# An empty 32 bytes in front of the late part's pool of a linear-attention and two-MLP kernel

## The chip, the core and the metric

The kernel runs on one core of one Trainium2 chip. The metric is the device time of one execution in microseconds (us); a kernel's time is the median over its runs.

## The reference

Attention with a feature map, then two MLPs (multi-layer perceptrons), all in float32. Inputs: q, k and v of 4 batches, 8 heads, 576 positions and 64 values; x below has 2,304 rows of 512.

```python
proj = x @ w_phi; proj -= max|proj|
phi = concat(exp(proj), exp(-proj))
attn = (phi(q) @ (phi(k).T @ v)) / (phi(q) @ sum(phi(k)) + 1e-6)
h = attn @ w_in;   g = where(h > 0, h, exp(min(h, 0)) - 1);   x = g @ w_out
h = x @ w_in2;     g = h * cos(h);                            out = g @ w_out2
```

Both MLPs go from 512 to 2,048 and back to 512.

## The kernel before, in words

**Work.** Attention fills `xy`, the 2,304 tokens as columns of 4 pieces of 128 partitions. The MLPs work on blocks of tokens: the first half of MLP 1 on blocks of 256 columns (the early part), its second half and all of MLP 2 on blocks of 384 (the late part). The late part is 6 blocks of 8 steps and 6 blocks of 16 steps, 144 steps in all. A step (`step`) takes 128 of the 2,048 hidden values: `g1` (L697) makes them with 12 matmuls, ACT and DVE put them through the activation, and `g2` (L705) adds them to the output banks with 12 more.

**Why 12 matmuls.** Each operand is split into a high part and a low remainder that TensorE takes in one pass each (`fp32r`); a product takes three passes (high by high, high by low, low by high) over 4 pieces. The stationary operand is a weight tile (`h` or `l`). The moving operand, the one that is streamed, is `x` in `g1` and `s` in `g2`, its high half in the first 384 columns of the tile and its low half in the next 384.

**Places in SBUF.** `unit` gives each kind of tile its places. `x` has 4 (`x0` to `x3`) and `s` three (`s0` to `s2`) in the pool `mp`. From the late part on, `s` has a fourth place, `sq0`, in the pool `mq`, and in MLP 2 from about 650 us on a fifth, `sx0`, in the pool `mx`. A step's `s` goes to whichever of them is free first by the plan. `mq` also holds three places for the activation's values (`gq`), two for what is loaded or stored at a block's end (`oq`) and two of `kq` (the whole number of turns for the cosine; a third, `kx0`, lies in `mx`). `swap("at", "wb", "mq")` releases attention's pool and opens `wb` and `mq` in its place, with `mq` behind `wb`.

In the built program, by the byte at which a tile starts in each partition: `mp` and `mx` come from the right-hand end of SBUF, and their tiles lie at 32 modulo 64 (`s0` at 216,032, `sx0` at 197,088, `x0` at 201,696, `kx0` at 200,160). `mq` begins at 174,912, and its tiles lie at 0 modulo 64 (`sq0` at 179,520). A tile of `x` or `s` takes 3,072 bytes, a half of it 1,536, so that both halves lie alike. The weight tiles and `xy` lie at 0 modulo 64.

**Order.** `plan` lists all instructions ahead of time from a table of costs and due times; each engine runs its own in that order. Addresses play no part in it.

Of the kernel before, what the change touches and what calls it, by code (L numbers as in the profile page):

```python
# [8 lines left out]
F32 = mybir.dt.float32  # L9
# [14 lines left out]
P = 128  # L24
# [46 lines left out]
NL, W1LATE, NEQ, EARLY = 4, -24.05, 4, 176.41  # L71
KLOAD, VLOAD, QSTEP = 20.0, 15.0, 4.0
NO = 2
JS, NSPLIT, WGAP = 4, 0, 20.0
ND, NKF, NVT, NQF, RAWB, NE = 5, 2, 2, 2, 4, 5

# [132 lines left out]
def bits(w):  # L209

    return w.bitcast(U32).rearrange("j p i (m t) -> j p i m t", t=2)
# [7 lines left out]
def body(tc, qt, kt, vt, wphi, w1, w2, out):  # L219
    nc = tc.nc  # L220
    pools, count = {}, itertools.count()

    def pool(name, **kw):
        pools[name] = tc.alloc_tile_pool(name=name, bufs=1, **kw)
        return pools[name]

    cst, xp, dr = pool("cst"), pool("xp"), pool("dr", space=DRAM)
    pool("wa")
    pool("wc")
# [1 line left out]
    pool("mp", side="right")  # L231
    pool("stg", side="right")
    pool("at")
    ws = {1: bits(w1), 2: bits(w2)}

    xy = xp.tile([P, NK, NT], F32, tag="xy", name="xy")
# [28 lines left out]
    def task(*args, **kw):  # L265
        t = Task(*args, **kw)
        t.ready = 0.0
        tasks.append(t)
        for b in t.bufs:
            if b.places[0][0] in hold:  # L270
                hold[b.places[0][0]].append(t)
        return t
# [4 lines left out]
    def unit(kind, late, last=False, dtype=F32):  # L277
        pool_of = {"x": {"mp": 4}, "s": {"mp": 3}, "g": {"mp": 2}, "o": {"mp": NO}, "k": {}}[kind]
        size = {"x": 2 * NB, "s": 2 * NB, "g": NA, "o": 2 * NA, "k": NB}[kind]
        places = [("mp", f"{kind}{i}") for i in range(pool_of.get("mp", 0))]  # L280
        if late and kind in "go":
            places, size = [], {"g": NB, "o": 2 * NB}[kind]
        if late:
            places += [("mq", f"{kind}q{i}") for i in range({"s": 1, "g": 3, "o": 2, "k": 2}.get(kind, 0))]
        if last:
            places += [("mx", f"{kind}x{i}") for i in range({"s": 1, "k": 1}.get(kind, 0))]
        return Buf(places, [P, size], dtype)
# [473 lines left out]
    def swap(old, *new, **kw):  # L761
        def fn():
            if old:
                pools[old].release()
            for n in new:
                pool(n, **kw)

        t = task("SP", 0.0, -1e6, fn, after=hold.get(old, hold["pools"]), latency=0.001)
        t.opens = new
        hold["pools"] = [t]  # L770
# [4 lines left out]
    for b in range(B):  # L775
        keys(b, BEGIN + PACE * (b * S / NA) - LEAD - KLEAD if b else 0.0, 4.0, reached)
        while T * P + P <= (b + 1) * S:
# [3 lines left out]
            T += 1  # L781
    end_a = BEGIN + BLOCK_A * (NT // NA)
    swap("at", "wb", "mq")
    for j in range(JA, NJ):
        convert("wb" if j > JA else "wc", 1, j, end_a + W1LATE + 4.0 * (j - JA) - (0 if j > JA else EARLY))
# [13 lines left out]
    for j in range(JA, NJ):  # L799
        convert("wb" if j > JA else "wc", 2, j, due + W2LATE + 4.2 * (j - JA))  # L800
    swap("stg", "mx", side="right")
    for c0, n in late:
        block(2, 0, c0, n, due, BLOCK_C * n / 384)
# [73 lines left out]
```

## Time and profile before

| | |
|---|---|
| median of 3 runs | 1008.83 us (1008.05 to 1008.95) |
| the profiled execution | 1008.61 us |
| its span, first to last instruction | 1006.7 us |
| granted TensorE clock | 1.000 |
| TensorE (PE) busy in the span | 994.3 us (99%) |
| VectorE (DVE), ScalarE (ACT), GpSimd (POOL) busy | 716.7, 504.4, 209.5 us |

The profile is of one execution. PE is the matmuls, PEld the loading of their stationary operand. Matmuls are pipelined: one starts before the last has ended, so that the time one takes (its duration, in ns) is longer than its distance to the next one's start.

### The profile page before, as it was taken

To read this page: it belongs to the slowest core of one execution; us is meant where nothing else is said; L and a number is where in the kernel's file an instruction comes from. 1 tells how busy PE (TensorE), PEld (TensorE's weight loads), DVE (VectorE), ACT (ScalarE), POOL (GpSimd) and SP (SyncE) were. 2 spreads that over 40 slices of the span, in tenths; PEclk is the share of its full clock that TensorE was granted. 3 is DMA by queue.
4 is the path that set the end of the run, shared out by engine and by line. 5 is a ranking of instruction groups with operands and counts; after the bars stand their busy time and mean duration, and the time that the engine had idled before them with its cause. 6 is when DMAs were issued, how large, how long until landed. Compare 5 with 4: busy or idle time off the path is not lost.

```text
span 1006.7 us, 21101 instructions
## 1 busy us (share of the span) xinstructions
PE 994.3 (99%) x8422; PEld 956.3 (95%) x8422; DVE 716.7 (71%) x1424; ACT 504.4 (50%) x1196; POOL 209.5 (21%) x262
## 2 busy tenths in 40 slices
PE   9999999999999999999999999999999999999998
PEld 6787988988999999999999999999999999999998
DVE  6999977778666678996444679975666666756564
ACT  6886753555456778875232576632232332422322
POOL 3556300000003447763000255500000000000000
PEclk9999999999999999999999999999999999999999
DMA  7544212120102345341002232100000000000000
GB/s 232 176 125 134 86 49 80 33 69 17 45 13 95 105 142 169 127 141 53 2 31 74 75 104 95 43 32 1 1 33 1 1 32 1 32 1 1 32 1 32
DMA packets 45889, 63.28 MB, mean 63 GB/s; under 512 B 5728, under 2 KB 24800, under 8 KB 45792
## 3 DMA queue, kind: packets, MB, share of 16 engines
q1 hardware_dynamic: 45632, 61.88, 19.5%
q8 instruction: 66, 1.08, 0.5%
q14 instruction: 31, 0.25, 0.1%
q10 hardware_dynamic: 160, 0.07, 0.0%
HBM read 52.49 MB, written 9.44 MB: 62 GB/s over the span
## 4 chain that ended last, share of the span: by engine, by line
PE 91%; DVE 5%; issue 1%; ACT 1%; POOL 1%; DMA 0%; DVEq 0%; ACTq 0%
PE h L697 24%; PE y L705 24%; PE a L697 15%; PE a L705 15%; PE a L561 4%; PE a L389 3%; PE a L441 3%; PE a L538 1%; DVE l L354 1%; DVE m L402 1%; DVE l L350 1%; DVE ek L470 1%; DVE d L405 1%; POOL l L358 1%; PE y L448 0%
## 5 line engine op out<-in xcount | busy, mean ns | idle before, releaser
L697 PE MATMUL h<-x,h 128*128 128x256 f32 (+1 forms) x1152 | 256.3, 313 | 0.1
L705 PE MATMUL y<-s,h 128*128 128x256 f32 (+1 forms) x956 | 205.0, 306 | 0.0
L697 PEld LDWEIGHTS h<-x,h 128*128 128x128 f32 x1152 | 192.8, 188 | 5.1 <-issue 3.3
L697 PE MATMUL h<-x,l 128*128 128x256 f32 (+1 forms) x576 | 178.6, 310 | 1.4 <-POOL l L372 1.4
L358 POOL TENSOR_TENSOR l<-l,h 128x256 int32<-128x256 int32 x128 | 105.1, 828 | 304.0 <-DMA raw<-w 190.6
L705 PEld LDWEIGHTS y<-s,h 128*128 128x128 f32 x956 | 157.2, 188 | 3.5 <-issue 1.9
L697 PE MATMUL a<-x,h 128*128 128x384 f32 x576 | 148.7, 340 | 0.0
L705 PE MATMUL y<-s,l 128*128 128x256 f32 (+1 forms) x478 | 145.2, 304 | 0.0
L372 POOL TENSOR_TENSOR l<-l,h 128x256 fp32r<-128x256 f32 x128 | 106.1, 838 | 134.3 <-ACT h L369 133.5
L697 PEld LDWEIGHTS h<-x,l 128*128 128x128 f32 x576 | 108.3, 188 | 1.6 <-POOL l L372 1.6
L739 ACT ACTIVATE gq<-gq,pihalf 128x384 f32<-128x384 f32 x96 | 59.2, 617 | 95.7 <-DVE gq L736 95.7
L697 PEld LDWEIGHTS a<-x,h 128*128 128x128 f32 x576 | 104.9, 188 | 0.0
L705 PE MATMUL a<-s,h 128*128 128x384 f32 x380 | 98.1, 340 | 0.0
L697 PE MATMUL a<-x,l 128*128 128x384 f32 x288 | 97.8, 340 | 0.0
L705 PEld LDWEIGHTS y<-s,l 128*128 128x128 f32 x478 | 89.9, 188 | 0.0
L369 ACT CAST h<-l 128x256 fp32r<-128x256 f32 x128 | 51.7, 406 | 37.6 <-POOL l L358 36.9
L354 DVE SCALAR_TENSOR_TENSOR l<-raw,l 128x256 uint32<-128x256 uint32 x128 | 69.1, 553 | 1.1
L705 PEld LDWEIGHTS a<-s,h 128*128 128x128 f32 x380 | 69.2, 188 | 0.0
L705 PE MATMUL a<-s,l 128*128 128x384 f32 x190 | 64.6, 340 | 0.0
L754 DVE TENSOR_TENSOR s<-gq,s 128x384 fp32r<-128x384 f32 x95 | 58.3, 613 | 3.5 <-ACT s L253 1.1
L343 ACT ACTIVATE l<-raw 128x256 f32<-128x256 f32 x128 | 56.0, 438 | 8.7 <-DMA raw<-w 8.5
L350 DVE TENSOR_SCALAR l<-l 128x256 uint32<-128x256 uint32 x128 | 51.2, 416 | 9.4 <-ACT l L343 8.2
(112 smaller groups left out, 1670.1 us busy)
## 6 DMA issues: line engine op xcount, KB each, us to landing
raw<-w SPq DMA_DIRECT2D x128, 256.0 KB, 3.0
qf<-qt SPq DMA_DIRECT2D x18, 256.0 KB, 2.7
part<-o SPq DMA_DIRECT2D x18, 256.0 KB, 2.4
oq<-part SPq DMA_DIRECT2D x12, 384.0 KB, 3.4
out<-oq SPq DMA_DIRECT2D x12, 384.0 KB, 2.5
kf<-kt SPq DMA_DIRECT2D x16, 256.0 KB, 3.6
vt<-vt SPq DMA_DIRECT2D x16, 256.0 KB, 2.8
kf<-kt SPq DMA_DIRECT2D x4, 128.0 KB, 3.3
```

The source lines that it names most:

```text
L343: nc.scalar.activation(f.tile, raw.tile[:, :, 1].bitcast(F32), AF.Copy, scale=2.0 ** -112)
L350: nc.vector.tensor_scalar(e, e, 3, None, ALU.logical_shift_left)
L354: nc.vector.scalar_tensor_tensor(e, raw.tile[:, :, 1], 0x80000000, e, ALU.bitwise_and, ALU.bitwise_or)
L358: nc.gpsimd.tensor_tensor(e, e, r.tile, ALU.add)
L369: task("ACT", cost(ACT_, CH), due, lambda: nc.scalar.copy(h.tile, f.tile), [h], [f])
L372: nc.gpsimd.tensor_sub(l.tile, f.tile, h.tile.bitcast(F32))
L389: nc.tensor.matmul(pp[odd].tile[0:r, i * NF:(i + 1) * NF], x.tile[rows, i, 0:r], ww[rows], start=(i == 0), stop=True, skip_group_check=True,)
L561: nc.tensor.matmul(ns[odd].tile[32 * h:32 * h + 32, g * P + lo:g * P + hi], k[:, half, h // 2, at:at + 32] if g < 2 else k[:, half, 2, 32 ...
L697: nc.tensor.matmul(hp.tile[:, 0:N], columns(W[m, j, 0, kk * P // CH][a], kk), xs[kk][c](), start=(kk == 0 and n == 0), stop=(kk == NK - 1 ...
L705: nc.tensor.matmul(yp(dt), columns(W[m, j, 1, dt * P // CH][a], dt), (hi, lo)[c](), start=(i == 0 and n == 0 and (late or dt % 2 == 0)), s ...
L739: nc.scalar.activation(g.tile[:, 0:N], g.tile[:, 0:N], AF.Sin, bias=pihalf)
L754: nc.vector.tensor_sub(lo(), g.tile[:, 0:N], hi().bitcast(F32))
```

## The change

A tile of 8 float32 values (32 bytes in each partition) that nothing writes or reads is allocated in `mq` when the pool is opened.

```diff
+SHIFTED = ("mq",)
...
+    def shift(name):
+
+        pools[name].tile([P, 8], F32, tag="pad", name=f"pad_{name}")
+
...
+    if "at" in SHIFTED:
+        shift("at")
...
             for n in new:
                 pool(n, **kw)
+                if n in SHIFTED:
+                    shift(n)
```

Since `SHIFTED` has `mq` alone, attention's pool gets no pad. In the built program all tiles of `mq` start 32 bytes later (`gq0` at 174,944, `sq0` at 179,552), and so at 32 modulo 64; every other tile is where it was. The instructions of each engine stand in the same order as before, row for row.

## Rows read from the trace of the kernel before

**Rows 1.** The page: head, busy time and share of the span, instructions.
```profile
span 1006.7 us, 21101 instructions
PE 994.3 (99%) x8422; PEld 956.3 (95%) x8422; DVE 716.7 (71%) x1424; ACT 504.4 (50%) x1196; POOL 209.5 (21%) x262
```
**Rows 2.** Busy time of each engine by stretch (us from the span's start).
```profile
core 0: us, PE busy (x) PEld busy (x) DVE busy (x) ACT busy (x) POOL busy (x), PEclk, DMA share, GB/s
...
401.00:650.00 249.00, 249.00 (x1414) 249.00 (x1413) 178.52 (x344) 141.19 (x350) 97.20 (x121) 1.00 0.24 78
650.00:990.00 340.00, 340.00 (x1929) 340.00 (x1929) 215.82 (x424) 105.72 (x201) 0.00 (x0) 1.00 0.04 12
990.00:1003.00 13.00, 12.76 (x73) 12.44 (x71) 5.73 (x11) 3.38 (x7) 0.00 (x0) 1.00 0.00 0
1003.00:1006.70 3.70, 0.00 (x0) 0.00 (x0) 0.00 (x0) 0.27 (x1) 0.00 (x0) 1.00 0.57 213
```
**Rows 3.** The chain that ended last, from 395 us on, shares by line.
```profile
by line: PE h L697 24.9%; PE a L705 24.9%; PE y L705 24.9%; PE a L697 24.7%; ACT oq L253 0.1%; issue 0.0%
```
**Rows 4.** Groups by form: busy us, mean ns of one; idle before them.
```profile
L697 PE MATMUL a<-x,h 128*128 128x384 f32 x576 | 148.7, 340 | 0.0
...
L705 PE MATMUL a<-s,h 128*128 128x384 f32 x380 | 98.1, 340 | 0.0
```
**Rows 5.** Tile `sq`: durations ns min/median/max, first and last start us.
```profile
L705 PE MATMUL a<-sq,h x128: 334/334/338, 401.6 to 994.9; 128*128 128x384 f32 x128
L705 PEld LDWEIGHTS y<-sq,h x128: 187/188/188, 402.5 to 995.7; 128*128 128x128 f32 x128
L705 PE MATMUL y<-sq,h x128: 334/334/334, 402.6 to 995.9; 128*128 128x384 f32 x128
...
L754 DVE TENSOR_TENSOR sq<-gq,sq x32: 546/559/1105, 398.2 to 985.1; 128x384 fp32r<-128x384 f32 x32
L255 DVE CAST sq<-gq x20: 359/360/361, 473.7 to 984.7; 128x384 fp32r<-128x384 f32 x20
```
**Rows 6.** Tile `sx`, the same view.
```profile
L705 PEld LDWEIGHTS y<-sx,h x68: 187/188/188, 658.5 to 997.8; 128*128 128x128 f32 x68
L705 PE MATMUL y<-sx,h x68: 337/340/342, 658.6 to 998.0; 128*128 128x384 f32 x68
...
L754 DVE TENSOR_TENSOR sx<-gq,sx x17: 551/557/559, 651.8 to 989.3; 128x384 fp32r<-128x384 f32 x17
L255 DVE CAST sx<-gq x14: 359/360/361, 651.4 to 988.9; 128x384 fp32r<-128x384 f32 x14
```
**Rows 7.** PE busy with matmuls of tile `sq` alone, two stretches, their sum.
```profile
395.00:600.00 205.00, 26.95 (x144) 1.00 0.26 84
600.00:1003.00 403.00, 44.93 (x240) 1.00 0.06 20
sum 608.00, PE 71.89; mean PE 35.94
```
**Rows 8.** The same for tile `sx`.
```profile
600.00:1003.00 403.00, 38.81 (x204) 1.00 0.06 20
```
**Rows 9.** Timeline of PE: start us, us, what; first of each `g2`.
```profile
994.15 0.51 PE L705 MATMUL a<-sq,h 128*128 128x384 f32 x2
...
996.24 0.52 PE L705 MATMUL a<-sx,h 128*128 128x384 f32 x2
...
998.36 0.52 PE L705 MATMUL a<-s,h 128*128 128x384 f32 x2
...
1000.48 0.52 PE L705 MATMUL a<-s,h 128*128 128x384 f32 x2
```
**Rows 10.** Tile `gq`: durations ns min/median/max, first and last start us.
```profile
L736 DVE SCALAR_TENSOR_TENSOR gq<-kq,gq x68: 544/559/1092, 597.5 to 991.3; 128x384 f32<-128x384 int32 x68
...
L736 DVE SCALAR_TENSOR_TENSOR gq<-kx,gq x28: 551/558/559, 652.9 to 995.5; 128x384 f32<-128x384 int32 x28
```
**Rows 11.** DMA issues: xcount, KB each, median us from issue to landing.
```profile
part<-o SPq DMA_DIRECT2D x18, 256.0 KB, 2.4
...
out<-oq SPq DMA_DIRECT2D x12, 384.0 KB, 2.5
```

## The prediction

> **What bounds the kernel now.** I read the busy times first. PE works for 994.3 of 1006.7 us [rows 1]; a busy PE alone says little, so the stretches come next. The change can act only once `mq` is in use, from about 395 us on. [...] So in the late part the end moves by what the distance from one matmul to the next changes, and by nothing else, save for the last 3.7 us, in which PE does nothing and the last store goes out [rows 2].
>
> **What the change does.** It adds and removes no instruction, wait or transfer, and moves none in its queue. It moves tiles by 32 bytes: `gq`, `oq`, `kq`, and the one place of `mq` that PE streams, `sq0`. So I go by kinds of access.
>
> *PE reads of `sq`.* The trace holds the comparison already, since the same code at the same line streams from `sq` (at 0 modulo 64) and from `s`, `sx` and `x` (at 32). From `x` and `s` one matmul of 384 columns takes 340 ns [rows 4], from `sx` 340 by the median, from `sq` 334 [rows 5, 6]. The weight loads take 188 ns in both [rows 5, 6], so the 6 ns are not theirs. Duration is not pace, though, because matmuls overlap; the pace is in the stretches. The matmuls of `sq` are 384 (32 groups `g2` of 12), and PE is busy with them for 71.89 us [rows 7]: 71.89 / 32 = 2.247 us a group. Those of `sx` are 204, 17 groups, in 38.81 us [rows 8]: 2.283 us a group. The difference is 0.036 us. Each stretch ends with the tail of its last matmul, which the next group overlaps, so I check it by starts: the `sq` group begins at 994.15 and the next at 996.24, 2.09 us; the `sx` group takes from there to 998.36, 2.12 us, and the `s` group behind it again 2.12 [rows 9]. That is 0.03 us, read to 0.01. The 32 groups then cost 32 x 0.030 = 1.0 us by the starts and 32 x 0.036 = 1.2 us by the stretches. I take **1.1 us, slower**. Ends for the range: 0 if the address is not what makes `sq` quick, and 384 x 6 ns = 2.3 us if all of the longer duration showed in the pace. I choose near the middle because the pace is measured directly and the duration is not a pace.
>
> All of it lies on the path, since PE has no idle time there to take it up [rows 2]. Nor does the mixture of both kinds of place cost anything that going uniform would give back: the `sx` group just behind the `sq` group takes the same 2.12 us as the `s` group behind another place at 32 [rows 9].
>
> [...]
>
> *DVE and ACT on `sq`, `gq`, `kq`.* Writing to a place at 0 or at 32 shows no difference: L754 takes 559 ns into `sq` and 557 into `sx`, L255 360 into both [rows 5, 6]. Nor do reads, as far as rows go: L736 takes 559 ns when it reads `kq`, at 0, and 558 when it reads `kx`, at 32 [rows 10]. ACT's reads of `gq` at 32 the trace does not show. Bounds: a saving of 6 ns an instruction to a loss of the same, as PE has it. I take 0, which DVE's rows are nearest to. What covers it is the lead of these engines over PE: DVE's last instruction for `sq` starts at 398.2 us at the first use and at 985.1 at the last, and PE starts reading at 401.6 and 994.15 [rows 5, 9]. Less the 0.56 us that the instruction takes, that is 2.8 and 8.5 us of lead; a step's chain has some eight instructions on the two engines, so a loss of 6 ns each would use 0.05 us of it. If that lead were gone, it would cost 0.05 us a step, 7 us over 144 steps; nothing in these rows brings it near that.
>
> *DMA on `oq`.* Fetches into `oq` land well ahead of use and only have DVE wait. The stores out of it are hidden too, but for the last, whose landing is in the final 3.7 us [rows 2]. A store from `oq` at 0 takes 2.5 us for 384 KB; one from `o`, which lies at 32, takes 2.4 us for 256 KB [rows 11]. Bounds for the last store: no cost if most of that is fixed, and if all of it went with the bytes, 2.4 x 384 / 256 = 3.6 us, 1.1 us more. I take 0, because 256 and 384 KB at almost the same time says that bytes are not what sets it.
>
> **The sum.** Profiled execution 1008.61 + 1.1 = 1009.7 us (span 1006.7 + 1.1 = 1007.8). The median of the runs stands 0.22 us above that execution, so I forecast 1008.83 + 1.1 = **1009.9 us**. That is 0.11% more, within the 0.2% (2.0 us) below which a measurement of this kernel hardly tells two versions apart.
>
> **Rivals.**
>
> *The place is innocent.* `sq0` differs from all other streamed places in more than its remainder: it lies at 179,520, the others at 197,088 and above. There is one such place in the trace, so the two readings can't be told apart there. If its quickness belongs to the region, or to some bank or end of the memory, 32 bytes don't take it away, `sq` stays at 334 ns, and the time is 1008.8 us. Against it: eight places at 32 in two pools (four of `x` and three of `s` in one, `sx` in the other) have the same 340 ns, so between those the region does not matter. [...]
>
> *Slower by the tail.* The change is to PE as forecast, and the last store is also slower from 32 modulo 64. Its place is the last 3.7 us, after PE has stopped, with nothing beside it. Its price is up to the 1.1 us worked out above, so 1008.83 + 1.1 + 1.1 = 1011.0 us, over the 0.2% bound. It decides from the point where the landing takes 0.9 us more than 2.5, that is 3.4 us. Against it: stores from `o`, at 32 already, land in 2.4 us [rows 11].
>
> [...]
>
> *Faster.* If PE's reads at 32 were slow because DVE and ACT work at 0 beside them, and `gq` at 32 took that away, the 340 ns would fall to 334 everywhere, and late PE time with it: 144 steps have 288 groups of 12, less the 32 that are quick already, 256 x 0.03 = 7.7 us, to 1001.1. Against it: at 998.36 to 1002.42, where DVE and ACT have little left (5.73 and 3.38 us in the last 13), an `s` group still takes 2.12 us [rows 2, 9].
>
> **How the numbers follow.** The forecast has 0.80, with a range of its own of 1009.2 to 1010.6 (1.1 us, give or take 0.2, and the spread of the medians, about 0.5). The innocent place has 0.13 at 1008.8, the slow tail 0.04 at 1011.0, the faster case 0.03. The range has to take in most of the first two cases and the upper bound in part: **1008.5 to 1010.8 us**. Slower by over 0.2% needs more than 1010.85: the tail's 0.04, and another 0.03 for the forecast's upper bound of 2.3 us and noise, 0.07. Faster by over 0.2% is 0.03. Within 0.2% is the rest, 0.90.
>
> **What would show it.** Right: in the changed kernel's profile the matmuls from `sq` take 340 ns by the median (337 to 342, as `sx` has it), the 32 groups some 73.0 us in place of 71.89, PE stays busy without a gap from 401 to 990 us, and the span grows by about 1.1 us, with the early 395 us, DVE's 559 ns and the landing of 2.5 us as they were. Wrong: `sq` still at 334 ns (the place is innocent), PE idle ahead of a `g2` (the lead of DVE or ACT was used up), a last store of over 3.4 us, or `s` and `x` at 334 ns.

## The result and the profile after

The changed kernel takes **998.36 us** (median of 5 runs, 998.03 to 998.64), the kernel before 1008.83 (1008.05 to 1009.12): a ratio of 0.9898, 95% interval [0.9888, 0.9909]. It is about 10.5 us faster. The forecast was 1009.9 us, slower by 1.1, in a range of 1008.5 to 1010.8: wrong in its sign and far outside the range.

The page of the changed kernel, the lines that answer to [rows 1] and to the DMA line of [rows 11]:

```profile
span 996.8 us, 21101 instructions
...
PE 983.3 (99%) x8422; PEld 945.2 (95%) x8422; DVE 715.2 (72%) x1424; ACT 504.8 (51%) x1196; POOL 210.3 (21%) x262
...
out<-oq SPq DMA_DIRECT2D x12, 384.0 KB, 2.5
```

The same number of instructions as before, DVE and ACT busy as long to within 1.5 us, and 11 us less of PE. Busy time by stretch, the changed kernel (answers to [rows 2]):

```profile
55.00:390.00 335.00, 330.14 (x4226) 303.22 (x4225) 263.59 (x537) 204.52 (x517) 81.04 (x94) 1.00 0.26 79
...
401.00:650.00 249.00, 249.00 (x1439) 249.00 (x1438) 180.81 (x349) 142.32 (x352) 97.20 (x121) 1.00 0.24 79
650.00:990.00 340.00, 340.00 (x1963) 340.00 (x1962) 218.29 (x429) 106.77 (x203) 0.00 (x0) 1.00 0.03 12
```

Read the counts, not the busy times. PE is busy for all of both late stretches before and after; but the same 249.00 us now hold 1,439 matmuls in place of 1,414, and the same 340.00 hold 1,963 in place of 1,929 [rows 2]. That is 249.00 / 1439 = 0.1730 us a matmul against 0.1761. The stretch from 55 to 390 us has 4,226 matmuls in both kernels. So the whole late part goes faster, not the matmuls of `sq`. The tiles show the same (durations ns min/median/max, first and last start). Changed kernel, tiles `x`, from 401 us on, and `sx` and `sq`:

```profile
L704 PE MATMUL a<-x,h x560: 335/336/338, 404.0 to 975.7; 128*128 128x384 f32 x187
...
L712 PE MATMUL y<-sx,h x68: 336/336/337, 654.6 to 988.1; 128*128 128x384 f32 x68
...
L712 PE MATMUL y<-sq,h x128: 333/336/338, 403.0 to 986.1; 128*128 128x384 f32 x128
```

`sq` went from 334 ns to 336, as little as that. What moved is `x`, `s` and `sx`, from 340 to 336, though their addresses are the same as before. Where that came from stands in the trace of the kernel before, in rows that the prediction does not use. Tile `x`, kernel before, first from 393.3 to 401.5 us and then from 403.7 us on:

```profile
L697 PE MATMUL a<-x,h x16: 335/336/336, 393.3 to 397.1; 128*128 128x384 f32 x16
L697 PE MATMUL h<-x,h x16: 336/336/336, 397.4 to 401.2; 128*128 128x384 f32 x16
...
L697 PE MATMUL a<-x,h x560: 337/340/342, 403.7 to 985.3; 128*128 128x384 f32 x187
L697 PE MATMUL h<-x,h x560: 337/340/342, 412.2 to 993.8; 128*128 128x384 f32 x187
```

The same tile at the same place is quick up to 401.5 us and slow from 403.7 on. Between the two lies the first group that streams from `sq`, at 401.6 us [rows 5]. The chain of waits of the kernel before, of which [rows 3] gives only the shares, has it too: a run of 24 matmuls takes 4.16 us ahead of that group, and 4.24 after it:

```profile
397.59 4.16 PE h L697 x24
...
425.00 4.24 PE a L697 x24
```

In the changed kernel such runs take 4.16 us to the end:

```profile
424.97 4.16 PE a L704 x24
...
788.97 4.16 PE a L704 x24
```

So there are two paces here, 4.16 / 24 = 173.3 ns and 4.24 / 24 = 176.7 ns from start to start. In the kernel before, the first group from `sq` switched the stream from the one to the other. The price: the late part has 288 groups of 12, less the 32 from `sq` and the 4 ahead of the first of these, which were quick already: 252, each 0.04 us shorter, 10.1 us. The two profiled executions are 998.64 and 1008.61 us, 10.0 apart, the medians 10.5.

### The profile page after: what moved, and what is told of

Same layout as the page of the kernel before. It is cut to its first block, busy times and chain, and to the rows that moved or that the text cites. A ratio compares the mean times of both kernels' runs of the same rounds, so it can differ in the third digit from the quotient of the medians.

```text
span 996.8 us, 21101 instructions
## 1 busy us (share of the span) xinstructions
PE 983.3 (99%) x8422; PEld 945.2 (95%) x8422; DVE 715.2 (72%) x1424; ACT 504.8 (51%) x1196; POOL 210.3 (21%) x262
## 4 chain that ended last, share of the span: by engine, by line
PE 91%; DVE 5%; ACT 2%; issue 1%; DMA 1%; POOL 1%; DVEq 0%; ACTq 0%
PE h L704 24%; PE y L712 24%; PE a L704 15%; PE a L712 15%; PE a L568 4%; PE a L396 3%; PE a L448 3%; PE a L545 1%; DMA kf<-kt 1%; DVE l L361 1%; DVE m L409 1%; DVE ek L477 1%; DVE d L412 1%; DVE l L357 1%; PE y L455 1%
```

## Experiments

Theory at first: **a kept pace** (a group from another kind of place upsets the stream for good). Rivals: **neighbours** (DVE and ACT at work on `gq`, `oq` and `kq` slow PE's reads), and **32 is the good place** (the remainder modulo 64 itself).

**Only `sq0` moved** (no pad at the start of `mq`):

```diff
+                    lone = b.place == ("mq", "sq0") and "lone" not in pools
+                    if lone:
+                        pools["mq"].tile([P, 8], F32, tag="pad1", name="pad_before")
                     b.tile = pools[b.place[0]].tile(
...
+                    if lone:
+                        pools["lone"] = None
+                        pools["mq"].tile([P, 8], F32, tag="pad2", name="pad_behind")
```

> Only sq0 moves to 32 modulo 64; gq, oq and kq stay at 0. Theory (a kept pace): as long as TensorE never pauses, matmuls of 384 columns from 32 go at 173.3 ns, until one from 0 comes in between, and after that at 176.7 ns to the end; so with sq0 at 32 nothing upsets the stream, all late matmuls go at 173.3 ns, 998.4 us. Rival (neighbours): DVE and ACT working on gq, oq and kq at 0 slow TensorE's reads at 32; they still do here and sq joins the slow ones, 1008.8 + 1.1 = 1009.9 us.

Measured: 998.09 us, ratio 0.9900 [0.9886, 0.9915]. With `gq0` and `oq0` where they were, and the other tiles of `mq` still at 0 modulo 64 (64 bytes further up), the whole gain is there.

**All but `sq0` moved** (the same edit on top of the change, so that `sq0` is at 179,584):

> The reverse: gq, oq and kq move to 32, sq0 stays at 0. Kept pace: 176.7 ns from the first group of sq on, at about 402 us, as before the change, 1008.8 us. Neighbours: 173.3 ns throughout, 998.4 us.

Measured: 998.06 us, ratio 0.9902 [0.9886, 0.9919]. The kept pace missed here, and the neighbours, which have this time right, missed in the run before. `sq0` is at 0 modulo 64 as before, but 64 bytes further up, and it upsets nothing. So, if the place of `sq0` is what counts, 64 is not the modulus. Since `sq0` moved in both runs, they do not show what moving `gq`, `oq` and `kq` alone would do.

**All streamed tiles at 0** (`SHIFTED` empty, a pad at the upper end of `mp`):

```diff
+    pools["mp"].tile([P, 8], F32, tag="pad", name="pad_mp")
     for name in ("mx", "mp", "ps", "mq", "wb", "wc", "wa", "xp", "dr", "cst"):
```

> An empty 32 bytes at the upper end of the pool mp instead, none in mq: x, s, sx, g, o and kx go to 0, where sq, gq, oq and kq are. Kept pace: what counts is that all streamed tiles lie alike, so the late part is at 173.3 ns, 998.4 us or, if the early part of 256 columns (117 to 118 ns a matmul now, 1728 of them) also gains up to 2 ns each, down to 995. Rival (32 is the good place): tiles at 0 are slow, 1008 us or more.

Measured: 1007.71 us, ratio 0.9996 [0.9986, 1.0005]; 1,419 matmuls in the stretch from 401 to 650 us. That is the rival's time, not the theory's: alike modulo 64 is not enough. That a place at 0 as such is slow does not stand either, after the run before.

**One matmul from 0** (in `g1`, ahead of one step; `here` is the MLP and the count of its steps so far, and the streamed tile is a weight tile):

```diff
...
+            if here == (2, 16):
+                moving = W[m, j, 0, 1][0].tile
+                nc.tensor.matmul(hp.tile[:, 0:CH], columns(W[m, j, 0, 0][0], 0), moving, start=True, stop=True)
```

> The changed kernel with one matmul more, ahead of the first step of the second block of the second MLP (about 665 us): 256 columns streamed from a weight tile at 0 modulo 64, into a bank that the next matmul overwrites. Kept pace: 173.3 ns before it, 176.7 ns from there to the end, some 1900 matmuls of 384 columns by 3.4 ns: 998.4 + 0.1 + 6.5 = 1005.0 us. Neighbours, or a cost paid by each matmul by itself: 998.4 + 0.1 = 998.5 us, with 173.3 ns on either side.

Measured: 998.04 us; 1,906 matmuls from 650 to 980 us, as in the kernel with only `sq0` moved. Behind it, at 655.0 us, the stream keeps its pace: by the starts 173.3 ns up to the next group of `sq` at 671.7. One matmul of 256 columns did not switch the pace.

**A new theory.** What the failed cases left is the place of the streamed tile relative to that of the weights, since the matmuls, which stream the one, and the weight loads, which take the other, run side by side: both are busy for 249.00 of 249.00 us [rows 2]. In the built programs all weight tiles lie at 64 modulo 256. The distance modulo 256 from there to the streamed tiles: before, `x`, `s` and `sx` 160, `sq` 0; in the changed kernel and with only `sq0` moved, `sq` 32; with all but `sq0` moved, 64; with all at 0, `x`, `s` and `sx` 128 and `sq` 0. To see PE by itself I put it alone on the chip, in a kernel that leaves out the computation (one execution): one loaded tile as weights and one as streamed operand, `at` being the distance in elements:

```python
w = wt[:, i % 8 * P:(i % 8 + 1) * P]
lo = cols * (i % 3 == 1)
nc.tensor.matmul(banks[i // 12 % 4][:, 0:cols], w, mv[:, at + lo:at + lo + cols],
                 start=(i % 12 == 0), stop=(i % 12 == 11))
```

> Not the computation: TensorE alone, 4,608 matmuls on one loaded tile, all weights at one remainder modulo 512, the streamed operand at a distance of d bytes from that, d = 0 to 480 by 32, with a short pause between series. Series: 48 matmuls of 384 columns for each d (first and last, twice in all); 24 at d = 160 (as x and s lie to the weights before), 12 at d, 36 at 160; 48 of 256 columns at each d; the same kicks from 128. Theory (two streams): the pace depends on d, and in a series at 160 on whether a group at another d came in between: the 36 after a kick by d = 0 (as sq lay before) go at 176.7 ns, after d = 32 and 64 (sq in the changed kernel and where all but sq moved) at 173.3, and series at 128 at 176. Rival (it takes the other engines): no difference by d, 173.3 ns in every series.

Mean distance from start to start in ns, worked out from the trace, over the last 24 or 36 matmuls of a series; two values where series at the same distance differed:

```
distance modulo 256                0       32            64      96      128     160     192     224
384 columns, one distance          173.33  173.33/176.67 173.33  176.67  175.54  173.33  173.33  173.33
384 columns at 160, after 12 at d  176.67  173.33        173.33  173.33  173.33  173.33  173.33  176.67
256 columns, one distance          120.00  117.79        117.79  120.00  118.54  117.33  113.33  118.33
```

The two paces of the kernel, 173.33 and 176.67 ns, came out of PE alone, with no other engine at work, so the neighbours are out. The pace depended on the distance, and distances 256 apart gave the same numbers (up to 0.05 ns, where there was one value). A stream at 160 was quick by itself in this run (173.33 ns); 12 matmuls at 0 or at 224 made it slow for all 36 that followed (176.67), and 12 at any other multiple of 32 did not (173.33). That is the kernel before (0), the changed one (32), and the one with all but `sq0` moved (64). A stream at 128 took 175.5 to 176.1 ns whatever 12 came in between, and the kernel with all at 0, whose `x` and `s` are at 128, takes 249.00 / 1419 = 175.5. The durations in the trace, tile `mv`: at 160 after 12 at distance 0, at 160 after 12 at 32, and 256 columns at 192:

```profile
L106 PE MATMUL b<-mv,wt x33: 337/338/342, 168.7 to 174.4; 128*128 128x384 f32 x33
...
L106 PE MATMUL b<-mv,wt x34: 334/336/337, 181.4 to 187.1; 128*128 128x384 f32 x34
...
L106 PE MATMUL b<-mv,wt x35: 276/276/276, 404.5 to 408.4; 128*128 128x256 f32 x35
```

A stall of PE, from the pause between series, stands near the start of each (two starts 342 and 285 ns apart behind the first slow one), and behind it the stream at 160 was quick again in this run (173.33 ns).

**`sq0` at 224 from the weights, and at 32 modulo 64** (the changed kernel with a larger pad):

```diff
-        pools[name].tile([P, 8], F32, tag="pad", name=f"pad_{name}")
+        pools[name].tile([P, 56], F32, tag="pad", name=f"pad_{name}")
```

> The changed kernel with an empty 224 bytes in place of 32: sq0 at 179,744, which is 32 modulo 64 as in the changed kernel, but 224 bytes modulo 256 from the weights (32 in the changed kernel, 0 before; x, s and sx: 160). Theory (distance to the weights modulo 256): a group at 224 turns a stream at 160 slow, as TensorE alone showed; x, s and sx at 176.7 ns from the first group of sq on, 1008.4 us, as before the change. Rival (all at 32 modulo 64 is what counts): 173.3 ns, 998.3 us.

Measured: 1008.54 us, ratio 0.9999 [0.9989, 1.0008], where the distance theory said 1008.4. By the words of the change (all streamed pieces at 32 modulo 64) this kernel is like the changed one, and it gains nothing. Its stretches, and the tiles `x` ahead of and behind the first group of `sq`:

```profile
401.00:650.00 249.00, 249.00 (x1415) 249.00 (x1414) 178.17 (x344) 143.10 (x354) 98.68 (x122) 1.00 0.24 80
```

```profile
L704 PE MATMUL a<-x,h x16: 335/336/337, 394.4 to 398.2; 128*128 128x384 f32 x16
...
L704 PE MATMUL a<-x,h x560: 335/338/342, 404.8 to 986.2; 128*128 128x384 f32 x187
```

**All streamed tiles at 192 from the weights**, the best distance for 256 columns with PE alone (113.33 ns):

```diff
-        pools[name].tile([P, 8], F32, tag="pad", name=f"pad_{name}")
+        pools[name].tile([P, 48], F32, tag="pad", name=f"pad_{name}")
...
-    pihalf = cst.tile([P, 1], F32, tag="pihalf", name="pihalf")
+    both = cst.tile([P, 2], F32, tag="pihalf", name="pihalf")
+    pihalf, eps = both[:, 0:1], both[:, 1:2]
...
-    eps = cst.tile([P, 1], F32, tag="eps", name="eps")
```

> pihalf and eps share one tile of cst, so that xy and all weights move 32 bytes down, and the pad in mq is 192 bytes: x, s, sx and sq all at 192 bytes modulo 256 from the weights. Distance theory: late part at 173.3 ns as in the changed kernel; early part at 113.3 ns in place of 117.8 (TensorE alone took 113.33 ns for 256 columns at 192, 117.33 at 160), 1728 matmuls by 4.4 ns = 7.7 us where nothing else is waited for: 990.7 us, at least below 995. Rival (all that counts is that streamed tiles lie alike): 998.3 us.

Measured: **995.9 us**, ratio 0.9870 [0.9853, 0.9886], faster than both kernels, though only by 2.5 us over the changed one, and not by 7.7. The late part has 1,439 matmuls from 401 to 650 us, as expected. In the early part the stretch from 55 to 390 us holds 4,246:

```profile
55.00:390.00 335.00, 330.65 (x4246) 303.73 (x4245) 267.42 (x542) 206.93 (x523) 81.76 (x95) 1.00 0.26 79
```

By the starts in its trace, of 1,627 unbroken distances at 256 columns 537 are at 113 or 114 ns and most others at 117 to 119; the mean is 116.4 ns against 117.7 in the changed kernel. 1,627 x 1.4 = 2.3 us, which is most of the gain. So 192 had two paces here as well, and the early part fell into either; what in it decides is not shown.

**PE alone, second run** (one execution): weights and streamed tile both 32 bytes further up, and finer steps.

> TensorE alone again, not the computation: weights and streamed tile both 32 bytes further up than in the first such run; series at distances from 128 to 256 by 8, for 384 and 256 columns, twice; at 192 with 12 matmuls at another distance in between; and series of 256 columns, then 384, then 256 at each distance by 32. Distance theory: the same paces as before at the same distances (384 columns: 128 175.5, 160 to 256 173.3; 256 columns: 128 118.5, 160 117.3, 192 113.3, 224 118.3, 256 120.0 ns), since only the difference counts; between the multiples of 32 open. Rival (the address itself counts): the paces of the series 32 bytes further up. Whether anything turns 192 slow is open.

At the same distances it gave the same paces: 256 columns 118.54, 117.38, 113.33, 118.33 and 120.00 ns at 128, 160, 192, 224 and 256; 384 columns 175.5 to 176.0 at 128, 173.33 at 224 and 256. So, as far as a shift of 32 bytes shows, the difference counts and not the address. It also gave what the first run had hidden: at 160 one series of 384 columns was at 173.33 ns and one at 176.67, and at 192 both such series were at 176.67, where the first run had 173.33. These two distances, and 32 in the first run, had more than one pace by themselves, and which one a series took was not the same each time. At 192 it depended on what came in between: streams of 384 columns came to 173.33 ns after 12 matmuls at 0 or 224, to 174.5 to 174.7 after 12 at 32, 64, 96 or 160, and to 176.67 after 12 at 128 or at 192 itself; streams of 256 columns came to 117.8 after 12 at 160 or 224, and else to 113.33. Distances between the multiples of 32 were no better: at 384 columns 208 came to 173.33 ns, the others to 174.7 to 180.0; at 256 columns they took 117.1 to 121.0.

**Is one visit enough, and what ends it?** Three more on the changed kernel. Twelve matmuls, ahead of one step:

```diff
...
+            if here == (2, 16):
+                for i in range(12):
+                    w = columns(W[m, j, 0, i % 4 // 2][0], i % 4)
+                    nc.tensor.matmul(hp.tile[:, 0:N], w, xb[i % 4].tile[:, 24:24 + N], start=(i == 0), stop=(i == 11))
```

> The changed kernel with 12 matmuls of 384 columns more, ahead of the first step of the second block of the second MLP (about 665 us), streamed from 96 bytes into the tiles of x, which is 0 modulo 256 from the weights; into a bank that the next matmul overwrites. Theory (distance, and a pace that is kept): 173.3 ns before them, 176.7 ns from there to the end, some 1880 matmuls less those of sq by 3.4 ns = 5.7 us, and 2.1 us for the 12: 998.3 + 7.8 = 1006.1 us. Rival (only matmuls near the group are slow, and sq had to come again and again): 998.3 + 2.1 = 1000.4 us.

The control has `64:64 + N` in place of `24:24 + N`:

> The control: the same 12 matmuls from 256 bytes into the tiles of x, so at 160 modulo 256 like x itself. Theory: nothing is upset, 173.3 ns throughout, 998.3 + 2.1 = 1000.4 us. Rival (any further group at that place upsets the stream): as with the 12 from 0, 1006.1 us.

And, besides the 12 from 0, a pause later:

```diff
...
+            if here == (2, 48):
+                w, rest = columns(W[m, j, 0, 0][0], 0), pools["mq"].tile([P, P], F32R, tag="rest", name="rest")
+                nc.tensor.matmul(hp.tile[:, 0:P], w, xs[0][0]()[:, 0:P], start=True, stop=True)
+                nc.scalar.copy(rest, hp.tile[:, 0:P])
+                nc.tensor.matmul(hp.tile[:, 0:P], w, rest, start=True, stop=True)
```

> The 12 matmuls from 0 at about 665 us, and at about 800 us, ahead of the fourth block of the second MLP, one pause of TensorE: a short matmul, a copy by ACT, and a short matmul that reads the copy. Theory: 176.7 ns between the two, 173.3 ns after the pause: 998.3 + 2.1 + 135 us x 0.019 = 2.6 + 1 to 2 for the pause, 1004 to 1005 us. Rival (a pause does not end it): 998.3 + 7.8 + 1 to 2, 1007 to 1008 us.

Measured: 1000.46, 1000.35 and 1001.02 us. By the times the first looks like the control, and the rival seems right. The tiles `x` in the first show that it is not:

```profile
L711 PE MATMUL a<-x,h x24: 337/340/343, 657.7 to 672.2; 128*128 128x384 f32 x24
...
L711 PE MATMUL a<-x,h x24: 335/337/337, 676.8 to 695.1; 128*128 128x384 f32 x24
```

The 12 did make the stream slow, `x` and `s` alike, from 657.7 us on. It stayed so for 17 us, until the next group from `sq`, at 674.7, and was quick behind it; the third kernel shows the same up to its group from `sq` at 674.0. The control shows it a third time, without any group at 0. In its trace the stream entered the late part slow, and was quick behind its first group from `sq`, at 401.3 us:

```profile
L711 PE MATMUL h<-x,h x16: 337/340/343, 397.0 to 400.9; 128*128 128x384 f32 x16
...
L711 PE MATMUL a<-x,h x558: 335/337/338, 403.9 to 977.1; 128*128 128x384 f32 x186
```

In the changed kernel `sq` lies at 32, and a group at 32 turned a slow stream quick again (340 ns ahead of it, 337 behind); in the kernel before it lay at 0, and the stream was slow behind each of its groups (2.12 us for every 12 matmuls). I had left that out: in the runs of PE alone, a pause always stood between the slow series and the next group. So in this kernel the slow pace costs 17 us x 0.019 = 0.3 us, too little to see in the time. The pause in the third kernel therefore came to a stream that was quick already, and says nothing about pauses. The forecasts of 1006.1 and of 1004 to 1005 us missed for the same reason.

## Why the prediction was wrong

- **What bounds the kernel** held: PE without idle time from 401 to 990 us, busy for all of the 249.00 and the 340.00 us, before and after.
- **No instruction, wait or transfer changes** held, as did the zeros for DVE (559 ns into `sq` before and after) and for the last store (2.5 us). The slow tail, at 0.04, did not come.
- **The term for the reads of `sq` failed.** "The trace holds the comparison already": I took the 0.036 us between a group from `sq` and one from `sx` for a property of the two places. But the pace of `x` and `s` was itself an effect of the groups from `sq` among them, so that I compared a cause with its consequence. With `sq` elsewhere, it was 252 other groups that moved, by 10.1 us, and not the 32 of `sq`, which were to cost 1.1 and have PE busy for 71.74 us in place of 71.89.
- **"Nor does the mixture of both kinds of place cost anything"** is where it could have been caught. I compared a group behind `sq` with a group behind `sx`, both at the end of the span and so both at the slow pace. The comparison that was needed is in time: `x` at 336 ns ahead of the first `sq`, 340 behind it.
- **The rival "the place is innocent"** (0.13) fell too: `sq` did not stay at 334 ns, and 1008.8 us is 10.4 too much.
- **The rival "faster"** (0.03) had the effect, though by luck, since its reason did not hold: 336 ns everywhere, `sq` within 2 ns of where it was, and 7.7 us of the 10.5. Its mechanism, DVE and ACT at 0 beside PE, fell with the run that moved `sq0` alone and with PE alone. Its size was short since it priced a group at 0.03 us, from `sq` groups of 2.09 us; the quick ones are 4.16 / 2 = 2.08, so 0.04.

What stays open: which of its paces a stream at 160 or 192 takes when it starts (173.33 or 176.67 ns at 384 columns), why 0 and 224 upset one at 160, and what makes the pace depend on the distance at all, 113.33 to 120.00 ns for 256 columns in the first run of PE alone. The kernel before and the changed one entered the late part quick in their traces, the control with the twelve from 160 slow; with PE alone the plain series of 384 columns at 192 were quick in the one run and slow in the other.

## What to carry to other kernels

Where PE has no idle time, divide a stretch by its count of matmuls, and follow that pace of one and the same tile through time before comparing it between tiles: here the step of tile `x` from 336 to 340 ns, behind the group at 401.6 us, named the event that caused it. With float32 matmuls of this kind, the remainder modulo 256 of the streamed tile's address less that of the weights is worth a look: here one odd buffer among nine set the pace of all others, 176.7 ns from start to start against 173.3. A small kernel with PE alone that sweeps the distance costs one run. From it the kernels with `sq0` at 224 and with the twelve from 160 were forecast to within 0.2 us; the other three were missed, all at 192 by 5.2 us and the two with the twelve from 0 by 5.6 and 3 to 4, because a distance had more than one pace (at 192, 256 columns took 113 or 114 ns or 117 to 119) and a group ended a slow one as well as started it (340 ns ahead of a group at 32, 337 behind).

## What was not expected of the hardware

- PE kept a pace: 36 matmuls in a row, and in the kernel 17 us, stayed at 176.7 ns after 12 matmuls at another distance, with nothing else changed, and one group at 32 brought back 173.3 ns, in three traces.
- With PE alone 256 columns took from 113.33 ns (distance 192) to 120.96 (152), 7% apart, and 384 columns from 173.33 to 180.00 (240), 4% apart, by the distance modulo 256. At 32, 160 and 192 series of 384 columns took 173.33 ns at one time and 176.67 at another.
